# Splitting loads by pairs of heads and reordering the first units of an attention and mixture-of-depths kernel

## Chip, cores and metric

The kernel runs on one core of a Trainium2 chip. The metric is device time in microseconds; a kernel's time is the median of several executions. One further execution was taken with the hardware profiler, and every view below is of that one.

## What is computed

Eight batches, eight heads, 576 positions, head size 64. The first block is linear attention; the second takes the 128 positions of each batch with the highest gate score through an MLP and adds the result, scaled by the sigmoid of the score:

```python
q_s = softmax(q, axis=-1)                 # over the 64 features
k_s = softmax(k, axis=2)                  # over the 576 positions
x = einsum(q_s, k_s^T v)                  # 'bhsd,bhde->bhse'
x = x.transpose(0, 2, 1, 3).reshape(B, S, 512)
scores = x @ w_gate
out = x.copy()
for b in range(B):
    top = argpartition(-scores[b], 128)[:128]
    h = relu(x[b, top] @ w1)              # 512 -> 1024
    out[b, top] += sigmoid(scores[b, top])[:, None] * (h @ w2)
```

All tensors are float32.

## The kernel before

**Units.** Work is cut into 16 units: a unit is four heads (`qd` 0 or 1) of one batch, so batch b is units 2b and 2b+1. For each unit q, k and v come in by `load`, each as two DMAs: one of 5 rows of 64 values for each of 64 partitions and four heads (320 KB), one of 4 rows (256 KB). There are three buffers per tensor (`LD = 3`), so a unit's load waits until the unit three before has been used up. All loads but v of unit 0 are issued on SP's queue; the stores of attention rows (`x_store`, two DMAs) and the weights (`load_w1` four times 512 KB, `load_w2` twice 1 MB) are issued there too, in the order of the program.

**Steps of a unit.** `k_exp` (ACT), `v_copy` (POOL or DVE, into a tile that has a column of ones beside v), `kv_mm` (40 TensorE matmuls), `q_exp` (ACT, two halves, the first for heads 0 and 1), `kv_out` (DVE reciprocal, ACT copy, and DVE product and sum with the gate weights `wg`), `q_t` (two times ten transposes, each evicted from PSUM by ACT with a scale), `x_mm` (80 matmuls), `x_out` (DVE: reciprocal, scaling into `xs`, and the score columns into `sr`), `x_store`.

**Steps of a batch.** `score` adds up the columns; `score_row` turns the scores into a row on all partitions (five TensorE transposes, ACT copies); `compare` ranks them with five DVE instructions; `pick` makes the list of the 128 rows (DVE, TensorE) and gathers them from the stored output by an indirect DMA on POOL (`xr`); `gate`; `turn` transposes the gathered rows (four TensorE transposes, an ACT copy into `xT`); `mlp1` in eight pieces (with a relu on ACT after the fourth and the eighth); `mlp2` in eight pieces; `finish` adds and scatters.

**Order.** The order on each engine is the order of the program (`tc.manual_schedule()`). An opening loop over s = 0 to 3 (`EARLY = 4`) does the attention of units 0 to 3 and, with `kv_mm` and the exps of unit s + 1, prepares unit 4 as well. `fill(n)` puts n matmuls of ones between, whose result is not used. Batch 0's score, compare, pick, gate and turn are part of this loop or follow it directly. The main loop runs over s = 4 to 19; its step s holds attention of unit s, `kv_mm` of unit s + 1, and MLP pieces of batch (s - 4) // 2: mlp1 in even steps, mlp2 in odd ones. The pieces fill TensorE between the steps of a unit: two after `q_t`, one after `kv_mm`, four after `score_row`, and in odd steps one more after the next batch's `turn`. In an odd step, `pick` of the next batch comes after the first two pieces, and `turn` of it after the following five.

Of the kernel before, what the change touches and what calls it, by code (L numbers as in the profile page):

```python
# [17 lines left out]
def kernel(  # L18
# [62 lines left out]
    def part(i):  # L81
        return slice(64 * i, 64 * i + 64)
# [6 lines left out]
    LD = 3  # L89
    raw = {w: [const.tile([P, 4, R, D], F32, name=f"{w}{n}") for n in range(LD)] for w in "qkv"}  # L90

    def load(u, which, queue=nc.sync):
        b, qd = units[u]
        for what in which:
            src = {"q": q, "k": k, "v": v}[what]
            t = raw[what][u % LD]
            first = src[b, 4 * qd].offset
            for n, rows in ((1, N2), (0, R)):
                queue.dma_start(
                    out=t[n::2, :, :rows].rearrange("p h r d -> p h (r d)"),  # L100
                    in_=bass.AP(tensor=src.tensor, offset=first + n * R * D,
                                ap=[[9 * D, 64], [SD, 4], [1, rows * D]]))
# [19 lines left out]
    wg = const.tile([P, NQ, 2, D], F32, name="wg")  # L122
    for h in range(2):
        nc.scalar.dma_start(out=wg[part(h)].rearrange("p a i d -> p (a i) d"),
                            in_=bass.AP(tensor=moe_w_gate.tensor, offset=moe_w_gate.offset + h * D,
                                        ap=[[0, 64], [2 * D, 2 * NQ], [1, D]]))
# [39 lines left out]
    rest = const.tile([P, B * R], I32, name="rest")  # L166
    nc.gpsimd.iota(whole.rearrange("p (b r) -> p b r", b=B), pattern=[[2 * S, B], [2, R]], base=0, channel_multiplier=9)
    nc.gpsimd.iota(odd_p, pattern=[[0, 1]], base=0, channel_multiplier=1)
    vals = const.tile([P, B, R, NV], BF16, name="vals")
    valid_r = const.tile([P, 3, R], F32, name="valid_r")  # L170
    s_all = const.tile([P, B, R], F32, name="s_all")
# [21 lines left out]
    def k_exp(u):  # L193
        ke = at.tile([P, 4, R, D], F32, tag="ke", name="ke")
        nc.scalar.activation(out=ke, in_=raw["k"][u % LD], func=AF.Exp)  # L195
        st["ke", u] = ke

    def q_exp(u, i):
        if i == 0:
            st["qe", u] = at.tile([P, 2, R, 2, D], F32, tag="qe", name="qe")  # L200
        qr = raw["q"][u % LD].rearrange("p (i h) r d -> p i r h d", i=2)
        nc.scalar.activation(out=st["qe", u][:, i], in_=qr[:, i], func=AF.Exp)  # L202

    def v_copy(u, engine=nc.vector):
        engine.tensor_copy(out=v_ones[u % 2][:, :, :, :D], in_=raw["v"][u % LD])
# [25 lines left out]
    def q_t(u, i):  # L231
# [10 lines left out]
        nc.scalar.activation(out=st["qT", u][:, i].rearrange("p r a c -> p a r c"),  # L242
                             in_=t_ps[:, :, :R * 64].rearrange("p a (r c) -> p a r c", r=R),
                             func=AF.Copy, scale=krec[:, u, i:i + 1])

    def x_mm(u, i):

# [8 lines left out]

    xs, sr = {}, {}

    def x_out(u, i):
# [4 lines left out]
        x = st.pop(("x", u, i))[:, :, :R * C].rearrange("p h (r c) -> p h r c", r=R)  # L264
        rec = qrec[:, u, i].rearrange("p (h r) -> p h r", h=2)
        nc.vector.reciprocal(out=rec, in_=x[:, :, :, D])  # L266
        nc.vector.tensor_mul(xs[b][:, :, qd, i].rearrange("p r h d -> p h r d"), x[:, :, :, :D],  # L267
                             rec.to_broadcast([P, 2, R, D]))
        nc.vector.tensor_mul(sr[b][:, 2 * qd + i].rearrange("p (h r) -> p h r", h=2), x[:, :, :, D + 1], rec)

    def x_store(u):
        b, qd = units[u]
# [132 lines left out]
    def each(step, b, *args):  # L405
        for n in range(n_sl):
            step(b, n, *args)
# [84 lines left out]
    def load_w1(n):  # L492
        nc.sync.dma_start(out=w1[:, n], in_=moe_w1[n * P:(n + 1) * P])

    def load_w2(n):
        half = KF // 2
        nc.sync.dma_start(out=w2[:, n * half:(n + 1) * half],
                          in_=moe_w2[n * half * P:(n + 1) * half * P].rearrange("(f p) d -> p f d", p=P))
# [20 lines left out]

    for s in range(EARLY):  # L520
        q_t(s, 0)
        q_t(s, 1)
        k_exp(s + 1)
        v_copy(s + 1, nc.gpsimd)
        fill(2)
        x_mm(s, 0)
        x_mm(s, 1)
        fill(2)
        if s == 2:
            kv_mm(s + 1)  # L530
            q_exp(s + 1, 0)
            fill(3)
            pick(0)
            x_out(s, 0)
            kv_out(s + 1)
            x_out(s, 1)
            x_store(s)
            q_exp(s + 1, 1)
        else:
            x_out(s, 0)  # L540
            x_out(s, 1)
            x_store(s)
            if s == 1:
                score(0)
            kv_mm(s + 1)
            q_exp(s + 1, 0)
            kv_out(s + 1)
            if s == 1:
                score_row(0)
                for r in range(R):  # L550
                    compare(0, r)
            q_exp(s + 1, 1)
            if s == 3:
                score(1)
        fill(2)
        if s == 0:
            load_w1(0)
            load_w1(1)
        elif s == 1:
            load_w1(2)  # L560
            load_w1(3)
            load(4, "kvq")
            load(5, "kvq")
        else:
            load_w2(s - 2)
            load(s + 4, "kvq")
    each(gate, 0)
    each(turn, 0)

    number = None  # L570
    for s in range(EARLY, NU + LAG):

        mlp_b, odd = divmod(s - LAG, 2)
        piece = mlp2 if odd else mlp1
        f_next = 0

        def pieces(n):
            nonlocal f_next
            for _ in range(n):
                each(piece, mlp_b, f_next)  # L580
                f_next += 1

        here = s < NU
        after = s + 1 < NU
        last = s == NU - 1
        ends = s // 2 if here and odd else None
        compared = s // 2 - 1 if here and not odd else None
        chosen = (s - 3) // 2 if here and odd else B - 1 if s == NU else None
        if here:
            q_t(s, 0)  # L590
            q_t(s, 1)
        if after:
# [64 lines left out]
```

## Time and profile before

| | us |
|---|---|
| median of 3 runs (218.0 to 220.29) | 218.38 |
| the profiled execution | 217.89 |
| its span | 216.00 |
| TensorE busy | 197.5 (91%) |
| DVE busy | 116.2 (54%) |
| ACT busy | 88.6 (41%) |
| POOL busy | 34.4 (16%) |
| first MLP matmul starts | 42.64 |
| last MLP matmul ends | 208.8 |

DMA moved 46.81 MB, of which 41.36 MB went by SP's queue. In 40 equal slices of the span (5.4 us each) the mean busy share of the DMA engines, in tenths, and the rate:

```
DMA  5999999999999997958594949421313041101001
GB/s 179 299 356 358 375 398 369 362 392 377 377 384 381 375 344 249 314 157 283 171 320 154 313 133 303 161 82 49 113 52 109 7 156 52 49 3 52 5 5 52
```

A row of the views reads: source line, engine, operation, tile written and tiles read, shape. In a row of a timeline, the brackets at the end hold the engine's idle time before the instruction and what released it; "issue" means that it waited for nothing that the profile shows. PE is TensorE's matmul, PEld its weight load, and an engine's name with a q is its instruction sequencer, which issues DMAs.

### The profile page before, as it was taken

To read this page: it belongs to the slowest core of one execution; us is meant where nothing else is said; L and a number is where in the kernel's file an instruction comes from. 1 tells how busy PE (TensorE), PEld (TensorE's weight loads), DVE (VectorE), ACT (ScalarE), POOL (GpSimd) and SP (SyncE) were. 2 spreads that over 40 slices of the span, in tenths; PEclk is the share of its full clock that TensorE was granted. 3 is DMA by queue.
4 is the path that set the end of the run, shared out by engine and by line. 5 is a ranking of instruction groups with operands and counts; after the bars stand their busy time and mean duration, and the time that the engine had idled before them with its cause. 6 is when DMAs were issued, how large, how long until landed. Compare 5 with 4: busy or idle time off the path is not lost. (4 is left out here: it accounts for less than half of the span.)

```text
span 216.0 us, 7090 instructions
## 1 busy us (share of the span) xinstructions
PE 197.5 (91%) x3040; PEld 147.2 (68%) x3040; DVE 116.2 (54%) x359; ACT 88.6 (41%) x146; POOL 34.4 (16%) x78
## 2 busy tenths in 40 slices
PE   5987595999999999999999999999999989999960
PEld 2464462799749975897679776996599548749620
DVE  6552595668726774477626872596358665501010
ACT  2386374763626471746265443536263311211100
POOL 6022402300112012200320023001120112101010
PEclk9999999999999999999999999999999999999996
DMA  5999999999999997958594949421313041101001
GB/s 179 299 356 358 375 398 369 362 392 377 377 384 381 375 344 249 314 157 283 171 320 154 313 133 303 161 82 49 113 52 109 7 156 52 49 3 52 5 5 52
DMA packets 39335, 46.81 MB, mean 217 GB/s; under 512 B 2944, under 2 KB 36736, under 8 KB 39296
## 3 DMA queue, kind: packets, MB, share of 16 engines
q1 hardware_dynamic: 36928, 41.36, 56.4%
q0 software_dynamic: 1280, 4.20, 5.7%
q10 hardware_dynamic: 1088, 0.72, 1.1%
q8 instruction: 26, 0.43, 0.8%
q14 instruction: 13, 0.11, 0.2%
HBM read 34.73 MB, written 11.53 MB: 214 GB/s over the span
## 5 line engine op out<-in xcount | busy, mean ns | idle before, releaser
L382 PE MATMUL mm<-xT,w 128*128 128x128 f32 x512 | 62.1, 278 | 0.0
L382 PEld LDWEIGHTS mm<-xT,w 128*128 128x128 f32 x512 | 58.8, 192 | 2.3 <-ACT xT L370 1.5
L392 PE MATMUL mm<-w,hT 128*128 128x512 f32 x128 | 59.9, 603 | 0.0
L315 DVE SCALAR_TENSOR_TENSOR junk<-srow,s,not_before 128x576 bf16<-128x576 f32 x40 | 32.8, 819 | 8.3 <-ACT srow L307 7.2
L392 PEld LDWEIGHTS mm<-w,hT 128*128 128x128 f32 x128 | 22.5, 190 | 21.2 <-issue 20.4
L267 DVE TENSOR_TENSOR xs<-x,qrec 128x640 f32<-128x640 f32 x32 | 26.4, 825 | 1.1
L242 ACT ACTIVATE qT<-x,krec 128x640 f32<-128x640 f32 x32 | 23.9, 792 | 6.2 <-PE x L239 6.1
L400 DVE SCALAR_TENSOR_TENSOR o<-mm,g,xr 128x512 f32<-128x512 f32 x8 | 6.0, 751 | 37.7 <-PE mm L392 37.7
L202 ACT ACTIVATE qe<-q 128x640 f32<-128x640 f32 x32 | 23.6, 739 | 3.0 <-DMA q<-in_q_dram 2.8
L215 PE MATMUL tp<-v_ones,ke 128*64 128x65 f32 x640 | 22.6, 224 | 2.3 <-issue 2.1
L215 PEld LDWEIGHTS tp<-v_ones,ke 128*64 128x64 f32 x640 | 20.3, 137 | 5.3 <-issue 3.0
L253 PE MATMUL x<-kv_w,qT 64*64 64x66 f32 x1280 | 22.4, 221 | 0.0
L347 POOL DMA_INDIRECT xr<-out_dram,idx x8 | 8.0, 996 | 88.8 <-DVE qrec L266 72.6
L253 PEld LDWEIGHTS x<-kv_w,qT 64*64 64x64 f32 x1280 | 20.2, 134 | 2.6 <-ACT qT L242 0.8
L195 ACT ACTIVATE ke<-k 128x1280 f32<-128x1280 f32 x16 | 20.3, 1270 | 2.8 <-DMA k<-in_k_dram 2.8
L385 ACT ACTIVATE hT<-mm 128x512 f32<-128x512 f32 x16 | 9.5, 596 | 28.7 <-PE mm L382 28.7
L239 PEld LDWEIGHTS x<-ident,qe 64*128 64x128 f32 x320 | 11.7, 139 | 11.6 <-issue 5.0
L239 PE MATMUL x<-ident,qe 64*128 64x64 f32 x320 | 14.5, 229 | 4.9 <-issue 1.4
L266 DVE RECIPROCAL qrec<-x 128x10 f32<-128x10 f32 x32 | 6.9, 215 | 20.7 <-PE x L253 20.7
L401 POOL DMA_INDIRECT out_dram<-o,idx x8 | 10.1, 1269 | 46.8 <-DVE o L400 46.8
L226 ACT COPY kv_w<-tp 128x130 f32<-128x130 f32 x16 | 4.3, 266 | 31.4 <-DVE krec L224 31.4
L370 ACT COPY xT<-mm 128x512 f32<-128x512 f32 x8 | 4.7, 585 | 26.9 <-PE mm L368 26.9
(81 smaller groups left out, 126.0 us busy)
## 6 DMA issues: line engine op xcount, KB each, us to landing
k<-in_k_dram SPq DMA_DIRECT2D x16, 320.0 KB, 7.0
q<-in_q_dram SPq DMA_DIRECT2D x16, 320.0 KB, 6.1
out_dram<-xs SPq DMA_DIRECT2D x16, 320.0 KB, 2.9
v<-in_v_dram SPq DMA_DIRECT2D x15, 320.0 KB, 7.9
k<-in_k_dram SPq DMA_DIRECT2D x16, 256.0 KB, 7.2
q<-in_q_dram SPq DMA_DIRECT2D x16, 256.0 KB, 6.4
out_dram<-xs SPq DMA_DIRECT2D x16, 256.0 KB, 3.2
v<-in_v_dram SPq DMA_DIRECT2D x15, 256.0 KB, 7.7
```

The lines of the kernel that those rows point to most:

```text
L195: nc.scalar.activation(out=ke, in_=raw["k"][u % LD], func=AF.Exp)
L202: nc.scalar.activation(out=st["qe", u][:, i], in_=qr[:, i], func=AF.Exp)
L215: nc.tensor.matmul(out=kv[part(h), i], lhsT=ke[:, 2 * i + h, r], rhs=vo[:, 2 * i + h, r], start=(r == 0), stop=(r == N2))
L239: nc.tensor.transpose(out=t_ps[:, a, r * 64:(r + 1) * 64], in_=qe[part(a), i, r].rearrange("p h d -> p (h d)"), identity=ident[part(a), pa ...
L242: nc.scalar.activation(out=st["qT", u][:, i].rearrange("p r a c -> p a r c"), in_=t_ps[:, :, :R * 64].rearrange("p a (r c) -> p a r c", r= ...
L253: nc.tensor.matmul(out=x[part(c), h, r * C:(r + 1) * C], lhsT=qT[part(h), i, r, c], rhs=kv_w[u % 2][part(h), i], start=True, stop=True)
L267: nc.vector.tensor_mul(xs[b][:, :, qd, i].rearrange("p r h d -> p h r d"), x[:, :, :, :D], rec.to_broadcast([P, 2, R, D]))
L315: nc.vector.scalar_tensor_tensor(junk, st["srow", b], st["s", b][:, r:r + 1], not_before[:, r], op0=OP.subtract, op1=OP.is_ge, accum_out=s ...
L382: nc.tensor.matmul(out=h_ps[:, f % 4 * m:(f % 4 + 1) * m], lhsT=w1[:, d, f * P:(f + 1) * P], rhs=xT[:, d, :m], start=(d == 0), stop=(d == ...
L385: nc.scalar.activation(out=hT[:, f - 3:f + 1, :m], in_=h_ps[:, :4 * m].rearrange("p (f c) -> p f c", f=4), func=AF.Relu)
L392: nc.tensor.matmul(out=st["y", b, n][:m], lhsT=st["hT", b, n][:, f, :m], rhs=w2[:, f], start=(f == 0), stop=(f == KF - 1))
L401: nc.gpsimd.indirect_dma_start(out=out_rows[:(b + 1) * S], out_offset=bass.IndirectOffsetOnAxis(ap=idx[:m, :1], axis=0), in_=o[:m], in_off ...
```

## The change

Six things are changed.

1. `load` splits each DMA by pairs of heads: four per tensor and unit instead of two (`parts=2`), for all units but 0 and 1, which keep two (`parts=1`). k of unit 0 goes by ACT's queue and SP's, one DMA each; v of unit 0 moves to SP. The gate weights `wg` move from ACT's queue to POOL's. `WARM` is 18 instead of 20.
2. `q_t` can evict on DVE; the second half of units 0 and 1 does.
3. `x_out` is made of `x_sums` (reciprocal and score columns) and `x_scale`. For unit 1 the score columns and `score(0)` come first, then the scaling.
4. Stores ahead of weights: `load_w1` follows the stores of both unit 0 and unit 1; then come load 4, `load_w2`, load 5, and later the store of unit 2, load 6, the store of unit 3.
5. The opening loop no longer prepares unit 4. `turn(0)` comes inside step 3, ahead of unit 3's `x_out`.
6. In main steps 4 and 5 four pieces come first, then the exp of k, the copy of v (on DVE) and `kv_mm` and the rest of that same unit, its load of s + 3, and one piece; the one and the four pieces later in the step are left out there. Step 5 also prepares unit 6, as before.

```diff
-    WARM = 20
+    WARM = 18
-    def load(u, which, queue=nc.sync):
+    def load(u, which, queues=(nc.sync, nc.sync), parts=2):
...
-            first = src[b, 4 * qd].offset
-            for n, rows in ((1, N2), (0, R)):
-                queue.dma_start(
...
+            for heads in range(0, 4, 4 // parts):
+                first = src[b, 4 * qd + heads].offset
+                for n, rows in ((1, N2), (0, R)):
+                    queues[n].dma_start(
+                        out=t[n::2, heads:heads + 4 // parts, :rows].rearrange("p h r d -> p h (r d)"),
+                        in_=bass.AP(tensor=src.tensor, offset=first + n * R * D,
+                                    ap=[[9 * D, 64], [SD, 4 // parts], [1, rows * D]]))
...
-    load(0, "k")
-    load(0, "v", nc.scalar)
-    load(0, "q")
-    load(1, "kvq")
+    load(0, "k", (nc.scalar, nc.sync), 1)
+    load(0, "vq", parts=1)
+    load(1, "kvq", parts=1)
     load(2, "kvq")
...
-        nc.scalar.dma_start(out=wg[part(h)]...
+        nc.gpsimd.dma_start(out=wg[part(h)]...
...
+        if on_vector:
+            nc.vector.tensor_scalar(to, src, krec[:, u, i:i + 1], None, op0=OP.mult)
+        else:
+            nc.scalar.activation(out=to, in_=src, func=AF.Copy, scale=krec[:, u, i:i + 1])
...
     for s in range(EARLY):
         q_t(s, 0)
-        q_t(s, 1)
-        k_exp(s + 1)
-        v_copy(s + 1, nc.gpsimd)
+        q_t(s, 1, on_vector=s < 2)
+        if s + 1 < EARLY:
+            k_exp(s + 1)
+            v_copy(s + 1, nc.gpsimd)
         fill(2)
         x_mm(s, 0)
         x_mm(s, 1)
         fill(2)
...
+        elif s == 1:
+            x_sums(s, 0)
+            x_sums(s, 1)
+            score(0)
+            x_scale(s, 0)
+            x_scale(s, 1)
+            x_store(s)
             kv_mm(s + 1)
             q_exp(s + 1, 0)
+            kv_out(s + 1)
+            score_row(0)
+            for r in range(R):
+                compare(0, r)
             fill(3)
+            q_exp(s + 1, 1)
+            for n in range(KD):
+                load_w1(n)
+            load(4, "kvq")
+            load_w2(0)
+            load_w2(1)
+            load(5, "kvq")
+        elif s == 2:
+            kv_mm(s + 1)
+            q_exp(s + 1, 0)
+            fill(2)
             pick(0)
             x_out(s, 0)
             kv_out(s + 1)
             x_out(s, 1)
             x_store(s)
             q_exp(s + 1, 1)
+            load(6, "kvq")
         else:
+            each(turn, 0)
             x_out(s, 0)
             x_out(s, 1)
             x_store(s)
...
+            score(1)
+            each(gate, 0)
+    late = EARLY, EARLY + 1
...
+        if s in late:
+            pieces(4)
+            k_exp(s)
+            v_copy(s)
+            kv_and_exp(s)
+            load(s + 3, "kvq")
+            pieces(1)
+        after = after and s + 1 not in late
...
-        if s + 4 < NU:
+        if after and s + 4 < NU:
             load(s + 4, "kvq")
-        pieces(1)
+        if s not in late:
+            pieces(1)
...
-        pieces(4)
+        if s not in late:
+            pieces(4)
```

More of the change, by code (lines that the diff above doesn't have):

```diff
@@ L96, in load @@
             t = raw[what][u % LD]
-            first = src[b, 4 * qd].offset
-            for n, rows in ((1, N2), (0, R)):
[L99 to L102, printed above, removed]
+            for heads in range(0, 4, 4 // parts):
[5 more added lines that the diff above has]
+                                    ap=[[9 * D, 64], [SD, 4 // parts], [1, rows * D]]))
     ctx.enter_context(tc.manual_schedule())
@@ L120 @@
         nc.tensor.matmul(out=w_ps, lhsT=ones_b[:, :P], rhs=ones_b, start=True, stop=True)
[L122 to L126, printed above, removed]
     warm = const.tile([P, 1], F32, name="warm")
@@ L168 @@
     nc.gpsimd.iota(odd_p, pattern=[[0, 1]], base=0, channel_multiplier=1)
+    wg = const.tile([P, NQ, 2, D], F32, name="wg")
+    for h in range(2):
+        nc.gpsimd.dma_start(out=wg[part(h)].rearrange("p a i d -> p (a i) d"),
+                            in_=bass.AP(tensor=moe_w_gate.tensor, offset=moe_w_gate.offset + h * D,
+                                        ap=[[0, 64], [2 * D, 2 * NQ], [1, D]]))
     vals = const.tile([P, B, R, NV], BF16, name="vals")
@@ L229, in kv_out, with q_t @@
         nc.vector.reduce_sum(out=kw[:, :, D + 1], in_=prod, axis=AX.X)
-    def q_t(u, i):
+    def q_t(u, i, on_vector=False):
         if i == 0:
@@ L241, in q_t @@
                                     identity=ident[part(a), part(a)])
-        nc.scalar.activation(out=st["qT", u][:, i].rearrange("p r a c -> p a r c"),
-                             in_=t_ps[:, :, :R * 64].rearrange("p a (r c) -> p a r c", r=R),
-                             func=AF.Copy, scale=krec[:, u, i:i + 1])
+        to = st["qT", u][:, i].rearrange("p r a c -> p a r c")
+        src = t_ps[:, :, :R * 64].rearrange("p a (r c) -> p a r c", r=R)
+        if on_vector:
+            nc.vector.tensor_scalar(to, src, krec[:, u, i:i + 1], None, op0=OP.mult)
+        else:
+            nc.scalar.activation(out=to, in_=src, func=AF.Copy, scale=krec[:, u, i:i + 1])
     def x_mm(u, i):
@@ L257, with x_view, x_sums @@
     xs, sr = {}, {}
-    def x_out(u, i):
+    def x_view(u, i):
+        rec = qrec[:, u, i].rearrange("p (h r) -> p h r", h=2)
+        return st["x", u, i][:, :, :R * C].rearrange("p h (r c) -> p h r c", r=R), rec
+    def x_sums(u, i):
         b, qd = units[u]
@@ L263, in x_out, with x_scale @@
             sr[b] = md.tile([P, NQ * 2, G], F32, tag="sr", name="sr")
-        x = st.pop(("x", u, i))[:, :, :R * C].rearrange("p h (r c) -> p h r c", r=R)
-        rec = qrec[:, u, i].rearrange("p (h r) -> p h r", h=2)
+        x, rec = x_view(u, i)
         nc.vector.reciprocal(out=rec, in_=x[:, :, :, D])
+        nc.vector.tensor_mul(sr[b][:, 2 * qd + i].rearrange("p (h r) -> p h r", h=2), x[:, :, :, D + 1], rec)
+    def x_scale(u, i):
+        b, qd = units[u]
+        x, rec = x_view(u, i)
         nc.vector.tensor_mul(xs[b][:, :, qd, i].rearrange("p r h d -> p h r d"), x[:, :, :, :D],
                              rec.to_broadcast([P, 2, R, D]))
-        nc.vector.tensor_mul(sr[b][:, 2 * qd + i].rearrange("p (h r) -> p h r", h=2), x[:, :, :, D + 1], rec)
+    def x_out(u, i):
+        x_sums(u, i)
+        x_scale(u, i)
     def x_store(u):
@@ L528 @@
         fill(2)
-        if s == 2:
+        if s == 0:
+            x_out(s, 0)
+            x_out(s, 1)
+            x_store(s)
+            kv_and_exp(s + 1)
+            fill(2)
[5 more added lines that the diff above has]
+            x_scale(s, 1)
+            x_store(s)
             kv_mm(s + 1)
             q_exp(s + 1, 0)
+            kv_out(s + 1)
+            score_row(0)
+            for r in range(R):
+                compare(0, r)
             fill(3)
+            q_exp(s + 1, 1)
[8 more added lines that the diff above has]
+            q_exp(s + 1, 0)
+            fill(2)
             pick(0)
@@ L542 @@
             x_store(s)
[L543 to L568, printed above, removed]
+            score(1)
+            each(gate, 0)
+    late = EARLY, EARLY + 1
     number = None
```

## The prediction, made before the changed kernel was run

> **What bounds the kernel now.** I read the stretches first, then the timeline up to the first MLP matmul, then the issue durations on SP. Stretches (length, then busy time of each engine with its count, granted clock, DMA share, GB/s):
>
> ```profile
> 18.00:26.00 8.00, 4.56 (x136) 3.35 (x132) 2.77 (x10) 3.05 (x4) 3.07 (x7) 1.00 1.08 365
> 34.00:42.00 8.00, 5.91 (x156) 4.39 (x158) 5.36 (x18) 5.16 (x9) 2.39 (x2) 1.00 1.08 363
> 42.00:54.00 12.00, 11.97 (x229) 11.45 (x225) 8.58 (x27) 6.48 (x14) 0.99 (x5) 1.00 1.07 382
> ```
>
> There are two regimes. Up to 42 us no engine is full and the DMA engines are: attention units 0 to 3 run at the pace of loads. From 42 us TensorE has no gap to the end. So the end moves by what the first MLP matmul (T0, 42.64 us here) moves, plus all TensorE work and every TensorE wait added after it.
>
> The timeline (start, duration, and in brackets idle time before it with its releaser):
>
> ```profile
> 25.56 0.33 PE L215 MATMUL tp<-v_ones,ke 128*64 128x65 f32 x3 [2.09 <-issue]
> 27.39 0.82 DVE L315 SCALAR_TENSOR_TENSOR junk<-srow,s,not_before 128x576 bf16<-128x576 f32 x1 [0.34 <-ACT srow L307]
> 33.97 1.17 POOL L347 DMA_INDIRECT xr<-out_dram,idx  x1 [7.55 <-DVE qrec L266]
> 41.24 0.60 PE L368 MATMUL mm<-ident,xr 128*128 128x128 f32 x4
> 42.64 2.05 PE L382 MATMUL mm<-xT,w 128*128 128x128 f32 x16
> ```
>
> The chain into T0 is: kv of unit 2, score row, five compares (27.39 to 31.6), hit, gather, turn, MLP. The gather is issued at 33.97 and its landing is the long piece: xr landings run from 3.3 to 6.2 us, and this one takes the whole 6.2 under full DMA.
>
> SP's issues (min/median/max ns):
>
> ```profile
> L99 SPq DMA_DIRECT2D q<-in_q_dram x32: 601/602/1079, 2.4 to 132.2; - x32
> L274 SPq DMA_DIRECT2D out_dram<-xs x32: 601/634/1776, 21.0 to 173.5; - x32
> L493 SPq DMA_DIRECT2D w<-in_moe_w_dram x4: 552/818/993, 22.6 to 26.7; - x4
> L497 SPq DMA_DIRECT2D w<-in_moe_w_dram x2: 397/496/596, 40.8 to 49.6; - x2
> ```
>
> An issue costs about 0.6 us whether it moves 256, 320 or 512 KB; the least is 0.40, for 1 MB. It doesn't follow size.
>
> [...] at 365 GB/s a 288 KB transfer takes 0.81 us, its issue 0.64; halved, 0.40 against 0.64. [...] The 2.09 us above (and 1.35 at 19.42) are TensorE waiting with nothing to wait for while DMA is full[...]. [...]
>
> **The change, part by part.**
>
> *Split loads.* A unit is 6 issues now, and in an unhindered stretch they take 1.32+1.28+1.26 = 3.86 us for k, v, q, or 0.64 each. From unit 2 on it is 12. If a half costs as much to issue, a unit takes 12 x 0.64 = 7.7 us of SP, against 1.77 MB / 365 GB/s = 4.85 us of DMA. So SP, not DMA, paces loads: about 230 GB/s. Bounds: 0.40 an issue (row L497; then DMA stays the limit) to 0.66. I take 0.64, because four kinds of transfer of different sizes sit at 0.55 to 0.64. [...]
>
> *SP's order up to T0.* Units 0 and 1 stay whole, and SP already waits for earlier transfers to land there (1.5 us for v at 5.6 to 7.1), so v of unit 2 can land near 18.5 us (3.67 MB through q of unit 1 at 14.4, two tensors more at 365 GB/s, 1 us to land) instead of the 20.3 at which POOL copies it now. The trace keeps SP about eight transfers ahead of the landings (7 us to land at some 0.8 us apart), so q of unit 2 is issued as k of unit 2 lands, from 15.6 on, and its last issue ends at 18.2. Unit 3 then ends at 26, the stores of units 0 and 1 (4 issues, moved ahead of w1) at 28.6, w1 at 31. Its 2.1 MB need 5.7 us: landed at 36 to 37 (34.5 now).
>
> *Chain to the pick.* Second evictions of units 0 and 1 on VectorE: 0.82 there (row L267 reads the same 128x640 from PSUM), beside an idle DVE (1.92 us idle before qrec), and 0.75 saved in ACT's serial pair. Score columns first: two xs multiplies (2 x 0.82) leave the path, but TensorE still does kv of unit 2 before the score row[...]. With unit 2 at 18.5, POOL's copy 1.25, kv at about 21 to 22.3, the row 1.4 more: compares start near 24.2 (27.39 now) and end at 28.5; hit 0.85, 1.4 to the issue: 30.8. The gather reads stored rows, and the stores land only about 30.8, so they agree. While w1 streams I take 5.8 us to land (3.9 to 6.2): 36.6. Turn and copy, 1.6 (41.03 to 42.64 now): **T0 = 38.2**, 4.4 earlier; bounds 36.0 and 40.0.
>
> *Work moved behind T0.* kv of unit 4 (1.39) and its transposes (0.84) are done before 42.64 now, and come after T0: +2.23. kv of unit 5 only moves inside the full stretch.
>
> *Three new TensorE waits.* (1) In step 4, four mlp1 pieces come first; the fourth emits the relu on ACT, and the exp of k of unit 4 stands behind it. TensorE goes straight to kv of unit 4, and idles for relu 0.60 + exp 1.27 + about 0.35 of signals = 2.2 us (1.9 to 2.4). v_copy of unit 4 moves from POOL to DVE (0.82), under that exp. (2) Step 5 wants kv of unit 5 after four mlp2 pieces (4 x 0.91), but its v_copy on DVE stands behind the five compares of batch 1. From the end of x_mm of unit 4: DVE finishes x_out after 1.7, compares 5 x 0.865 = 4.3, copy 0.82, signal 0.15: 7.05. TensorE has score row 0.71, a piece 0.93, four pieces 3.65: 5.3. Wait 1.75 (1.4 to 2.1). (3) In step 5 the turn of batch 1 now follows the pick after only x_mm 1.40 and kv of unit 6 1.39, since the one and four pieces between them were used up earlier. From the pick's matmul: 1.4 to the gather's issue, 3.9 to 4.3 to land, against 0.27+1.40+1.39 = 3.06: wait 2.6 (1.7 to 4.7, landing 3.3 to 6.2). Behind the turn stand the last piece, finish, and all of step 6. Nothing recovers this, TensorE being full afterwards.
>
> *Costed at nothing.* wg through POOL: two issues at 4 to 6 us, beside loads; wanted at 11.37 by prod; without that cover up to 1 us on unit 0, which then waits for unit 1's loads anyway. Two warm matmuls fewer and k of unit 0 on two queues: k lands sooner, but DVE's v_copy starts at 7.50 behind constants as now. Loads 7 and 8 issued later: at 7.7 us a unit SP has unit 5 out by 47 and unit 6 by 56, wanted from about 56 on; unit 7 by 65, wanted at 73. In the steady stretch 12 x 0.64 + 1.3 = 9.0 us fit into 11.4. Moving w2 behind load 4: out by 40, wanted at 52.
>
> **Sum:** (38.2 - 42.64) + 2.23 + 2.2 + 1.75 + 2.6 = +4.3 us. The profiled execution is 217.89 (span 216.00 and 1.89 around it), so 222.2. The median of runs shown, 218.38, is 0.5 higher; I leave that.
>
> **Rivals.**
> - *The start is worth more than I give it (faster).* [...] If halves cost 0.40 to issue [...], bytes alone allow w1 at 31.4 (7.2 MB of loads, 1.2 of stores, 2.1 of w1 at 365 to 370 GB/s from 2.2 us, and 0.8), the gather is issued at 27 and lands at 30.9: T0 = 32.5. With wait (3) at 1.7: -10.1 + 2.23 + 2.2 + 1.75 + 1.7 = -2.3: 215.6. It decides the sign when T0 falls below 33.9. For it: the two waits on issue. Against: no issue of 256 to 512 KB took under 0.55.
> - *Gain and waits cancel.* T0 = 35.5 (issue near 0.5), waits at their low ends 1.9+1.4+2.0: -7.1 + 2.2 + 5.3 = +0.4: 218.3.
> - *The waits cost more.* T0 = 40 (gather issued at 32.5 and landing in 6.2), waits 2.4 + 2.1 + 4.0: +8.1: 226. [...]
> - *It doesn't do what it says:* the queues run in program order in this trace, so the moved steps move; no chance given.
>
> **Numbers.** My forecast has 0.47, the costly case 0.18, cancellation 0.22 and the faster start 0.13. Faster by over 1% (what these runs can tell from no change) needs under 216.2: 0.13. Slower by over 1% is over 220.6: forecast and costly case, and a little of the third: 0.67. Within: 0.20. The range runs from 217, below the cancelling case, to 226; it leaves out the faster start and the top of the costly case.
>
> **What would show it.** Issue rows of half loads at 0.6 us and DMA share below 0.9 between 20 and 30 us; the first mlp1 matmul near 38; in step 4 TensorE idle before kv, released by ke; in step 5 idle before kv, released by DVE's v_ones, and again before the turn, released by the landing of xr. I'm wrong if halves issue in 0.4 or less, if T0 is under 34, or if the waits are not there, because the engines' order differs from the program's.

## The result, and the profile after

The changed kernel takes 235.68 us (median of 4, 233.83 to 237.28) where the kernel before, run beside it, takes 219.33: a ratio of 1.0735, 95% interval 1.061 to 1.086. It is slower, as forecast, but by 16 us instead of 4. The profiled execution took 237.28 us, the longest of the four, with a span of 235.5.

Granted clock and DMA share in 40 equal slices of the span, in tenths:

```profile
PEclk9999997679999589999999999999999999999995
DMA  6996799799888798799969876997723130111001
```

Before, the clock was full until 212 us and the DMA row stood at 9 from 5 to 81 us. Now DMA is no longer full throughout, and TensorE falls to half clock twice between 36 and 50 us (for 3.41 us from 35.95 and for 6.83 from 42.78) and again from 77 to 84 (6.83 us from 76.91). The same three stretches as before (length, busy time and count of PE, PEld, DVE, ACT, POOL, clock, DMA share, GB/s):

```profile
18.00:26.00 8.00, 6.56 (x162) 4.60 (x164) 6.04 (x18) 4.84 (x9) 2.24 (x6) 1.00 0.66 181
34.00:42.00 8.00, 4.38 (x102) 3.25 (x104) 4.56 (x16) 2.38 (x4) 1.36 (x3) 0.79 0.99 344
42.00:54.00 12.00, 7.49 (x60) 6.93 (x62) 1.14 (x3) 3.07 (x5) 0.71 (x4) 0.72 0.84 270
```

From 18 to 26 us the loads move 181 GB/s; it was 365. TensorE, which had no gap from 42 us on, is busy for 7.49 of the 12 us after 42. The timeline of SP's queue shows what the loads wait for (start, duration of the group, count):

```profile
23.54 3.04 SPq L101 DMA_DIRECT2D v<-in_v_dram  x4
26.68 2.60 SPq L101 DMA_DIRECT2D q<-in_q_dram  x4
29.38 2.92 SPq L289 DMA_DIRECT2D out_dram<-xs  x4
32.34 2.98 SPq L508 DMA_DIRECT2D w<-in_moe_w_dram  x4
35.42 3.48 SPq L101 DMA_DIRECT2D k<-in_k_dram  x4
...
56.91 3.38 SPq L101 DMA_DIRECT2D q<-in_q_dram  x4
60.38 1.31 SPq L289 DMA_DIRECT2D out_dram<-xs  x2
...
67.17 3.31 SPq L101 DMA_DIRECT2D q<-in_q_dram  x4
70.58 1.31 SPq L289 DMA_DIRECT2D out_dram<-xs  x2
```

One group follows the other within 0.6 us, and mostly 0.1, from 17 to 80 us: SP has no time to spare. Until 36 us and after 58 almost all of it goes into the issues themselves. In between, the groups are longer than their issues: four half loads of v take 4.85 us from 51.96, and for 2.2 us of that (54.0 to 56.2) SP waits for transfers that it issued earlier. The stores of units 0 and 1 leave at 29.4, w1 at 32.3, and the store of unit 3 only at 70.6; before it was 46.4. What this does to the first batch, in the timeline of all engines:

```profile
29.43 1.25 POOL L206 COPY v_ones<-v 128x1280 f32<-128x1280 f32 x1 [7.08 <-DMA v<-in_v_dram]
30.73 1.39 PE L216 MATMUL tp<-v_ones,ke 128*64 128x65 f32 x40 [2.70 <-POOL v_ones L206]
32.50 0.27 PE L354 MATMUL tp<-vals,hit 128*128 128x5 bf16 x5
37.20 1.07 POOL L362 DMA_INDIRECT xr<-out_dram,idx  x1 [6.52 <-DVE xs L279]
43.99 1.09 PE L383 MATMUL mm<-ident,xr 128*128 128x128 f32 x4 [3.56 <-DMA xr<-out_dram,idx]
```

The compares ran from 24.23 to 28.50 and hit was there at 29.36. But the pick's matmul (32.50) stands behind kv of unit 3 (30.73), which waits for v of unit 3. Then the list is ready at 33.15, and the gather still isn't issued until 37.20, because the rows that it reads were stored late: the last store of unit 1 landed at 36.32. (The brackets name an instruction of DVE that writes `xs` for a later unit, which the gather doesn't read. POOL's queue had waited for the four stores until 36.32; with the stores on another queue, below, the gather follows its list.) From the first MLP matmul on, TensorE's own timeline has these waits, and one of 1.1 us near the end:

```profile
45.75 5.66 PE L397 MATMUL mm<-xT,w 128*128 128x128 f32 x32 [0.67 <-ACT xT L385]
53.26 1.39 PE L216 MATMUL tp<-v_ones,ke 128*64 128x65 f32 x40 [1.84 <-ACT ke L196]
66.69 1.39 PE L216 MATMUL tp<-v_ones,ke 128*64 128x65 f32 x40 [1.85 <-DVE v_ones L206]
80.26 1.12 PE L383 MATMUL mm<-ident,xr 128*128 128x128 f32 x4 [5.71 <-DMA xr<-out_dram,idx]
```

After the 0.67 us before T0 itself, they are the three that the prediction named, in its order and with its releasers. The 5.66 us of the first 32 matmuls, which take 3.84 at full clock in the run with whole loads below, are the low clock.

### The profile page after: what moved, and what is told of

Its sections match the earlier page's. It is cut to its first block, busy times and chain, and to the rows that moved or that the text cites. A ratio compares the mean times of both kernels' runs of the same rounds, so it can differ in the third digit from the quotient of the medians.

```text
span 235.5 us, 7207 instructions
## 1 busy us (share of the span) xinstructions
PE 199.3 (85%) x3026; PEld 150.0 (64%) x3034; DVE 119.1 (51%) x362; ACT 87.5 (37%) x144; POOL 34.5 (15%) x79
## 5 line engine op out<-in xcount | busy, mean ns | idle before, releaser
L397 PE MATMUL mm<-xT,w 128*128 128x128 f32 x512 | 64.2, 283 | 0.7 <-ACT xT L385 0.7
L397 PEld LDWEIGHTS mm<-xT,w 128*128 128x128 f32 x512 | 60.7, 197 | 3.2 <-ACT xT L385 2.4
L407 PE MATMUL mm<-w,hT 128*128 128x512 f32 x128 | 61.0, 610 | 0.0
L248 ACT ACTIVATE qT<-x,krec 128x640 f32<-128x640 f32 x30 | 22.4, 790 | 7.3 <-PE x L240 7.3
L257 PE MATMUL x<-kv_w,qT 64*64 64x66 f32 x1280 | 23.3, 225 | 0.3
L257 PEld LDWEIGHTS x<-kv_w,qT 64*64 64x64 f32 x1280 | 21.1, 138 | 3.2 <-ACT qT L248 1.5
```

The costliest lines, as they stand in the source:

```text
L248: nc.scalar.activation(out=to, in_=src, func=AF.Copy, scale=krec[:, u, i:i + 1])
L257: nc.tensor.matmul(out=x[part(c), h, r * C:(r + 1) * C], lhsT=qT[part(h), i, r, c], rhs=kv_w[u % 2][part(h), i], start=True, stop=True)
L397: nc.tensor.matmul(out=h_ps[:, f % 4 * m:(f % 4 + 1) * m], lhsT=w1[:, d, f * P:(f + 1) * P], rhs=xT[:, d, :m], start=(d == 0), stop=(d == ...
L407: nc.tensor.matmul(out=st["y", b, n][:m], lhsT=st["hT", b, n][:, f, :m], rhs=w2[:, f], start=(f == 0), stop=(f == KF - 1))
```

## Experiments

The theory after this reading: the split is the main loss. It makes SP's issues the pace, and everything queued on SP (stores, w1, the loads of later units) comes late; the three waits of the late place of units 4 and 5 add some 6 us. The rival: the new place of units 4 and 5 is the loss, and the split only feeds it. All kernels ran beside the kernel before, in sets of their own. In the last two sets (late_pick_first, w2late_fills, before_opening, and then pick_turn_first) the kernel before itself took 224.3 to 224.4 us, in the others 219.3 to 220.0, so between sets only ratios are compared.

| run | us | ratio to before (95%) | first MLP matmul |
|---|---|---|---|
| changed kernel | 235.7 | 1.074 (1.061 to 1.086) | 45.75 |
| whole_late | 228.1 | 1.038 (1.031 to 1.045) | 42.54 |
| split_old | 234.1 | 1.064 (1.057 to 1.072) | 50.85 |
| whole_old | 224.7 | 1.022 (1.013 to 1.031) | 46.64 |
| split_late_fills | 234.4 | 1.066 (1.055 to 1.076) | 46.03 |
| whole_old_w2late | 221.6 | 1.011 (1.000 to 1.021) | 43.89 |
| before_split | 232.4 | 1.059 (1.051 to 1.067) | 51.71 |
| split_late_poolstores | 232.9 | 1.060 (1.048 to 1.071) | 43.14 |
| whole_late_tuned | 225.1 | 1.024 (1.014 to 1.035) | 43.03 |
| late_pick_first | 234.7 | 1.043 (1.036 to 1.050) | 40.36 |
| w2late_fills | 224.6 | 0.998 (0.995 to 1.000) | 43.85 |
| before_opening | 224.1 | 1.001 (0.998 to 1.004) | 44.93 |
| pick_turn_first | 225.4 | 1.006 (1.004 to 1.009) | 43.29 |

### The split and the late place, crossed

By the late place the kernel is meant whose units 4 and 5 are prepared inside the MLP, by the old one that in which the opening loop prepares unit 4.

whole_late is the changed kernel with whole loads:

```diff
-    def load(u, which, queues=(nc.sync, nc.sync), parts=2):
+    def load(u, which, queues=(nc.sync, nc.sync), parts=1):
```

> The changed kernel with parts=1 everywhere: loads are whole again, all else as changed. Theory A (the split is the larger cost: SP's issue of 0.60 us per half paces loads, so v of unit 3, the stores and w1 come late, with them both gathers, and TensorE idles long enough to lose its clock): first mlp1 matmul near 38.5 us (45.75 in the changed kernel), v of unit 3 copied by 27, the gather of batch 1 issued within 0.5 us of its idx (3.5 after it in the changed kernel), 221 to 224 us. Theory B (the order with kv of units 4 and 5 inside the MLP is the larger cost, through its three TensorE waits): 229 us or more.

split_old keeps the split and puts unit 4 back into the opening loop; whole_old has both edits.

```diff
-        if s + 1 < EARLY:
-            k_exp(s + 1)
-            v_copy(s + 1, nc.gpsimd)
+        k_exp(s + 1)
+        v_copy(s + 1, nc.gpsimd)
...
         else:
-            each(turn, 0)
             x_out(s, 0)
             x_out(s, 1)
             x_store(s)
+            kv_and_exp(s + 1)
+            load(s + 4, "kvq")
             score(1)
+            fill(2)
             each(gate, 0)
+            each(turn, 0)
...
-    late = EARLY, EARLY + 1
+    late = ()
```

> The changed kernel with split loads, but with unit 4 prepared in the opening loop, turn(0) after it and main steps 4 and 5 in the order of the kernel before. Theory A: no TensorE wait within steps 4 and 5, but the first mlp1 matmul at 47 to 50 us, since kv of unit 4 waits for v of unit 4 (landed at 46.8 in the changed kernel); 225 to 229 us. Theory B: 222 us or less.

> Both of the two edits undone: whole loads, and units 4 and 5 in the order before; what is left are the two eviction engines, score columns first, stores ahead of weights, wg on POOL. Theory A: 8 to 12 us under split_old. Theory B: at most 3 us under split_old, and well under whole_late. Both: first mlp1 matmul at 39 to 41.5 us and 214.5 to 217 us, under the kernel before, as nothing of this part costs TensorE time later.

Taking the split away gains 7.6 us with the late place (235.7 to 228.1) and 9.4 with the old one (234.1 to 224.7). Taking the late place away gains 1.6 with the split, where the intervals of the two ratios overlap, and 3.4 without it. So the split is the larger part in both orders. whole_late fits neither of its theories, 221 to 224 or 229 and more: its v of unit 3 is copied by 25.6, as expected, but its first MLP matmul comes at 42.54 and not near 38.5. Without the split the compares start at 26.53 again, the pick (33.20) still stands behind kv of unit 3, and the gather takes 7.0 us to land. split_old missed its 225 to 229: with unit 4 in the opening loop TensorE stands 7.09 us for the v of unit 4 and 5.31 at kv of unit 5, since the split loads bring them late. The late place covers much of that. whole_old missed its 214.5 to 217 too, and this is the first sign of another loss: with both parts undone, 5.2 us remained.

### The split alone, in the kernel before

```diff
-    def load(u, which, queue=nc.sync):
+    def load(u, which, queue=nc.sync, parts=2):
...
+            for heads in range(0, 4, 4 // parts):
...
-    load(1, "kvq")
+    load(1, "kvq", parts=1)
```

> The kernel before with one edit: the loads of units 2 to 7 are split by pairs of heads, everything else stays. Theory A: the split costs by itself, since an issue takes 0.6 us whether it moves 128 or 256 KB, so SP paces the loads and a unit takes 7.2 to 8.7 us instead of 4.9: 226 us or more, with TensorE waiting for k or v of units 3 to 5. Rival B: the split only hurts because the stores and w2 were put in its way by the other parts of the change: at most 221.

It is theory A: one edit, ratio 1.059. The edit splits all loads from unit 2 on, as the changed kernel does, and not those of units 2 to 7 alone. The stretches of this kernel (first, and third of the three):

```profile
18.00:26.00 8.00, 7.20 (x179) 4.83 (x180) 5.38 (x17) 5.58 (x9) 2.24 (x6) 1.00 0.71 197
...
42.00:54.00 12.00, 7.73 (x94) 6.58 (x98) 2.26 (x9) 6.23 (x9) 2.24 (x6) 0.58 0.81 234
```

and its issues of q loads on SP (min/median/max ns):

```profile
L100 SPq DMA_DIRECT2D q<-in_q_dram x60: 601/605/1247, 2.4 to 161.4; - x60
```

Before, whole loads issued in 601/602 ns. Half the bytes issue in the same time, so 12 issues hold SP for 7.3 us or more (12 x 0.605), and from 18 to 26 us DMA runs at 197 GB/s and a share of 0.71, where the kernel before has 365 GB/s and 1.08. Timeline of SP's queue in the same run:

```profile
27.72 1.32 SPq L275 DMA_DIRECT2D out_dram<-xs  x2
29.09 1.49 SPq L494 DMA_DIRECT2D w<-in_moe_w_dram  x2
30.68 2.92 SPq L275 DMA_DIRECT2D out_dram<-xs  x2
33.64 1.43 SPq L494 DMA_DIRECT2D w<-in_moe_w_dram  x2
35.17 2.62 SPq L100 DMA_DIRECT2D k<-in_k_dram  x4
37.89 3.35 SPq L100 DMA_DIRECT2D v<-in_v_dram  x4
```

The store of unit 0 goes at 27.7 (21.0 before) and v of unit 4 at 37.9 (29.3 before). The list of batch 0 is ready at 31.21, sooner than the 33.68 of before, as the first loads do land sooner. But the gather is issued at 39.03, a microsecond after the last store of unit 1 landed (38.04), and v of unit 4 lands only at 45.0; its kv starts at 46.3 (39.5 before), and TensorE's turn follows at 49.5. What the split wins for unit 2 it loses several times over on everything that is queued behind it.

### The stores, and the pick behind kv

First the stores of units 0 to 5 on POOL's queue, then also the pick ahead of kv of unit 3:

```diff
-            nc.sync.dma_start(
+            (nc.gpsimd if u < 6 else nc.sync).dma_start(
```

> The changed kernel with one edit: the stores of units 0 to 5 are issued on POOL's queue instead of SP's. Theory A: in the changed kernel the stores stand behind twelve split loads on SP (the store of unit 3 is issued at 70.6 us, the gather of batch 1 only after it has landed, at 75.8, although its indices are there at 72.3). It expects the gather of batch 0 to be issued at 33.5 to 34.5 (37.2 in the changed kernel), the gather of batch 1 within about 1 us of its indices, the wait of TensorE for it to fall from 5.7 to about 2.6 to 3 us, and 227 to 231 us. Rival B: stores are not what the gathers wait for, or POOL's queue only moves the wait: 234 to 237.

```diff
+            pick(0)
             kv_mm(s + 1)
             q_exp(s + 1, 0)
             fill(2)
-            pick(0)
```

> The changed kernel with the stores of units 0 to 5 on POOL's queue (232.9, first MLP matmul at 43.14 us) and one more edit: the pick of batch 0 stands ahead of kv of unit 3 on TensorE instead of behind it. Theory A: in the changed kernel the pick was ready at 29.4 and stood until 32.5 behind a kv that waited for v of unit 3, and this is one of the two things that made the first MLP matmul late, the stores being the other. It expects the pick at 29.5 to 30.5, the gather issued at 31 to 32 and landed at 37 to 38; the turn then waits for the x matmuls of unit 3 and no more for the gather, so the first MLP matmul comes at 40 to 41.5, and the time is 229.5 to 231.5. Rival B: v of unit 3 sets the pace anyway, because the x matmuls of unit 3 stand ahead of the turn and end at 41 to 42 whatever the pick does: first MLP matmul at 42.5 or later, 232 to 234.

The gathers do what was expected of theory A. Timeline of split_late_poolstores:

```profile
34.93 1.06 POOL L362 DMA_INDIRECT xr<-out_dram,idx  x1 [4.16 <-DVE qrec L273]
...
69.14 0.28 PE L354 MATMUL tp<-vals,hit 128*128 128x5 bf16 x5 [1.77 <-DVE hit L350]
...
74.62 0.65 PE L383 MATMUL mm<-ident,xr 128*128 128x128 f32 x4 [2.37 <-DMA xr<-out_dram,idx]
```

The gather of batch 0 follows its list by 0.3 us, and the third wait falls from 5.71 to 2.37 us, near the 2.6 of the prediction. The time, 232.9, lies between the two expectations, and the interval of its ratio overlaps that of the changed kernel; 1.77 us comes back as a new wait of the pick of batch 1 for hit, and the pick of batch 0 comes later than in the changed kernel (33.9 after 32.5). With the pick first as well, TensorE's timeline of late_pick_first reads:

```profile
29.39 0.28 PE L354 MATMUL tp<-vals,hit 128*128 128x5 bf16 x5 [1.38 <-DVE hit L350]
30.50 1.58 PE L216 MATMUL tp<-v_ones,ke 128*64 128x65 f32 x40 [0.83 <-POOL v_ones L206]
...
39.08 0.60 PE L383 MATMUL mm<-ident,xr 128*128 128x128 f32 x4
40.36 3.84 PE L397 MATMUL mm<-xT,w 128*128 128x128 f32 x32 [0.68 <-ACT xT L385]
```

The gather is issued at 30.61, where the prediction had 30.8, but lands only at 38.18. The first MLP matmul comes at 40.36: 5.4 us of its delay were the two places where something stood in a queue. The ratio of 1.0433, put on the kernel before of the earlier set (219.96), is 229.5, the lower end of what was expected of theory A; its interval just overlaps that of split_late_poolstores (1.048 to 1.071). As the two runs are of different sets, only the time of the first matmul is compared between their traces.

### The clock

```diff
+            fill(10)
             kv_mm(s + 1)
             q_exp(s + 1, 0)
             fill(2)
             pick(0)
+            fill(6)
...
+            fill(14)
             each(turn, 0)
```

and 24 more matmuls of ones before the turn of batch 1.

> The changed kernel with unused matmuls of ones where TensorE idles: 10 before kv of unit 3, 6 after the pick of batch 0, 14 before turn(0), 24 before the turn of batch 1 (0.21 us each at full clock). They keep TensorE busy and leave what it waits for. If the slow clock is a cost of its own (mlp1 took 5.66 us for 32 matmuls of the profile where 3.7 is the rate at full clock): granted clock 1.00 until the end, 231 to 232.5 us. If not: no change, 234 to 237 us.

Within the work the clock is then full but for one stretch, 46.3 to 49.7, in which the first MLP matmuls still take 5.47 us; its mean over the span is 0.987 instead of 0.953. The rest after them is 2.4 us shorter in the traces, the median 1.3 us, less than its uncertainty. The median is where no change was expected (234 to 237). So the slow clock accounts for a microsecond or two, not for the loss.

### The three waits

whole_late_tuned is whole_late with w2 where the kernel before has it, and in steps 4 and 5 of the main loop the exp of k and the copy of v (on POOL) ahead of the pieces; in step 5 one piece stands ahead of kv, and three are kept for the time before the turn.

```diff
         if s in late:
-            pieces(4)
             k_exp(s)
-            v_copy(s)
+            v_copy(s, nc.gpsimd)
+            pieces(1 if odd else 4)
...
+        elif odd:
+            pieces(3)
```

> The run with whole loads and the new place of units 4 and 5 (228.1), with two things altered: w2 back where the kernel before has it, and in the first two steps of the main loop the exp of k and the copy of v (on POOL again) stand ahead of the MLP pieces instead of behind four of them, with pieces left over for the time before kv and before the turn of batch 1. Theory A: the three new waits (exp of k behind the relu, v copy behind five compares, turn right behind the pick) are what the new place costs, and w2 early costs the start: the waits fall to at most 1 us together, the first MLP matmul comes at 41 to 42.5, and the time is 219 to 222. Rival B: the waits only move to other places, or w2 isn't the cause of the late start: 225 to 229.

```profile
56.83 1.39 PE L216 MATMUL tp<-v_ones,ke 128*64 128x65 f32 x40 [1.03 <-issue]
```

Wait 1 is gone. In place of wait 2 TensorE stands 1.03 us before kv of unit 5: the exp of its k, which comes after a relu on ACT, ends only 0.1 us before that kv starts. A further 0.68 us goes to an exp of q, and the third wait is 1.26 us instead of 2.17. Together that is 2.97 us where whole_late has 1.85 + 1.75 + 2.17 = 5.77, and not the 1 us expected. From the first MLP matmul to the end it took 180.2 us instead of 183.4. So the waits cost some 3 us that another order of the same work saves, if none of it is w2's. The first MLP matmul stayed at 43.0, though, with the pick behind kv of unit 3 again (33.42), and 225.1 is what Rival B expected. It doesn't reach whole_old_w2late below, which has the old place of units 4 and 5.

### What remained: w2, the dummy matmuls, the rest of the opening

whole_old_w2late moves w2 back:

```diff
             load(4, "kvq")
-            load_w2(0)
-            load_w2(1)
             load(5, "kvq")
...
+            load_w2(0)
             load(6, "kvq")
...
+            load_w2(1)
             load(s + 4, "kvq")
```

> The run with whole loads and the old place of unit 4 (224.7, first MLP matmul at 46.6 us), with w2 put back where the kernel before has it: its first half after the query exponentials of unit 3, ahead of load 6, its second half one opening step later, ahead of load 7. Theory A: what was left of the loss (+5.2 us against the kernel before) is w2's 2 MB taking the DMA engines at 34 to 42 us[...]. It then expects the gather of batch 0 to land in about 6.2 us instead of 7.8, the first MLP matmul at 41 to 42.5, and 217 to 220 us. Rival B: w2 is not the cause (the new order of stores, weights, evictions or the gate weights on POOL is): 223 to 226, first MLP matmul at 45 or later.

It took 221.6, 3.1 us less than whole_old (the intervals of the ratios overlap, 1.013 to 1.031 and 1.000 to 1.021). The time lies between the two expectations, and the first MLP matmul moved by 2.8 us, not by the 4 or 5 expected. In whole_old TensorE's timeline has

```profile
37.62 1.32 PE L257 MATMUL x<-kv_w,qT 64*64 64x66 f32 x73
41.24 0.34 PE L257 MATMUL x<-kv_w,qT 64*64 64x66 f32 x7 [2.30 <-issue]
...
42.43 2.44 PE L216 MATMUL tp<-v_ones,ke 128*64 128x65 f32 x40
```

with a wait for nothing that the profile shows in the middle of 80 matmuls, then kv at half clock. With w2 late that wait is gone, the gather lands in 7.1 instead of 7.8 us, and v of unit 5 is copied by 44.8 instead of 50.4. So w2's place carries most of this remainder by the traces; what the 2.30 us waited for isn't shown.

In two more runs, w2late_fills puts back dummy matmuls of the kernel before around the pick, and before_opening is the kernel before with only the evictions on VectorE and the score columns first.

```diff
-            fill(2)
+            fill(3)
             pick(0)
...
             q_exp(s + 1, 1)
+            fill(2)
             load_w2(0)
```

> The run with whole loads, the old place of unit 4 and w2 late (221.6, first MLP matmul at 43.89 us) with the dummy matmuls of the kernel before put back around the pick of batch 0: three instead of two ahead of it and two behind it. Theory A: without these two TensorE was idle for 1.7 and 1.1 us with 0.5 us of work between, fell to half clock from 34.3 to 41.2, and the x matmuls, fills and kv of units 3 and 4 took 2.2 us longer. It expects a clock of 1.00 to the end, the first MLP matmul at 41.3 to 42.3, and 219 to 220.3 us. Rival B: the clock doesn't matter there, since the turn waits for something else [...]: first MLP matmul at 43 or later, 221 to 222.5.

> The kernel before with two parts of the change alone: the second eviction of units 0 and 1 on VectorE, and in the second opening step the sums and the score columns ahead of the two multiplies of xs, which come before the store. Theory A: these parts do what the prediction gave them, the compares start some 1 us earlier than 27.4 us and the gather is issued that much earlier; since it lands 6.2 to 7 us later and kv of unit 4 and the fills stand ahead of the turn, little of it reaches the first MLP matmul: 41.5 to 42.6 us, and 217.5 to 219.5, no change that can be told. Rival B: they gain as much as they move, the gather lands at 39 and the first MLP matmul comes by 41.3: 216 to 217.3. Rival C: a later store of unit 1 holds the gather back: above 220.

before_opening is at 1.001: these two parts, made alone, change nothing that can be told. The way to it was not the one expected: the compares start at 27.28, hardly sooner than the 27.39 of before, and the first MLP matmul comes at 44.93, not at 41.5 to 42.6. w2late_fills is at 0.998, level with the kernel before, so what is left of the change costs nothing on balance once the split, the place of units 4 and 5, w2 and these dummy matmuls are undone. The parts left, stores ahead of w1 and the gate weights on POOL among them, weren't run one by one. The expected mechanism isn't shown, however: its profiled run still had half clock from 36.1 to 39.5, and its first MLP matmul at 43.85. That the dummies are worth the last per cent rests on two ratios from different sets.

The last run tried to beat both kernels by moving TensorE's order on from w2late_fills:

```diff
+            pick(0)
+            fill(2)
             kv_mm(s + 1)
             q_exp(s + 1, 0)
-            fill(3)
-            pick(0)
...
             x_store(s)
+            each(turn, 0)
             kv_and_exp(s + 1)
...
-            each(turn, 0)
```

> The run with w2 late and the fills put back (0.998 of the kernel before), with two moves on TensorE: the pick of batch 0 ahead of kv of unit 3, and the turn of batch 0 ahead of kv of unit 4. Theory A: in that run the pick stood 1.7 us behind kv of unit 3 (hit 31.2, pick 32.95) and the turn stood 2 us after the gather had landed (40.5, 42.45) behind kv of unit 4 and two fills; taken away, this brings the gather's issue to 32.3 and its landing to 39, the first MLP matmul comes before or right after kv of unit 4, and the time falls by 1 to 2.5 us, to a ratio of 0.988 to 0.996 against the kernel before: faster, by little. Rival B: TensorE's order was not the limit there, since what moves ahead only pushes kv back and TensorE does the same work after it: ratio 0.996 to 1.003. Rival C: with the pick first TensorE waits for hit ahead of kv of unit 3, and the delay of kv of units 3 and 4 costs more than the gather gains: above 1.003.

```profile
31.59 0.28 PE L354 MATMUL tp<-vals,hit 128*128 128x5 bf16 x5 [1.39 <-DVE hit L350]
...
39.68 0.63 PE L383 MATMUL mm<-ident,xr 128*128 128x128 f32 x4 [0.59 <-DMA xr<-out_dram,idx]
40.24 1.39 PE L216 MATMUL tp<-v_ones,ke 128*64 128x65 f32 x40
...
43.29 2.05 PE L397 MATMUL mm<-xT,w 128*128 128x128 f32 x16
```

The lines are TensorE's timeline of pick_turn_first. The gather is issued at 32.54 and landed at 39.54, as expected, but TensorE now stands 1.39 us for hit and 0.59 for the gather, and does kv of unit 4 after the turn instead of before it. The ratio is 1.006 (1.004 to 1.009): Rival C. No version run here is shown to beat the kernel before.

## Why the prediction went wrong

By its steps, against the profiled execution (237.28 us, 15.1 above the predicted 222.2). T0 is the start of the first MLP matmul.

| step | predicted | measured | adds to 222.2 |
|---|---|---|---|
| the issue of a half load, us | 0.64 | 0.60 to 0.64 | |
| compares start, end | 24.2, 28.5 | 24.23, 28.50 | |
| gather of batch 0 issued | 30.8 | 37.20 | |
| first MLP matmul (T0) | 38.2 | 45.75 | +7.6 |
| wait 1, exp of k behind the relu | 2.2 | 1.84 | -0.4 |
| wait 2, v copy behind the compares | 1.75 | 1.85 | +0.1 |
| wait 3, turn of batch 1 | 2.6 | 5.71 | +3.1 |
| low clock after T0 | none | 3.5 | +3.5 |
| TensorE waits for DVE near the end (206 us) | none | 1.1 | +1.1 |

The low clock is worked out as 5.66 - 3.84 us for the first 32 MLP matmuls, plus 1.70 for the turn of batch 1 (1.12 for 0.60), two mlp2 pieces (1.92 for 1.02) and the transposes after them (1.12 for 0.84). The moved work is 1.39 and 0.84 us in this trace too, the 2.23 of the prediction. The rows add up to 15.0 of the 15.1.

**What was right.** The direction; that an issue doesn't follow size, so that SP paces the loads; unit 2 earlier and the compares to within 0.1 us; the three waits with their places and releasers, two of them within 0.4 us. (The terms of wait 2 add up to 7.0 and not 7.05, so it was 1.7 by its own sum. The 0.35 us of signals in wait 1 was an estimate: in the trace the relu starts 0.04 us after the matmuls, kv 0.05 after the exp, and the exp 0.1 before the relu ends.) The early compares came with the split: they start at 24.00 in before_split, and at 27.28 with the evictions and the score columns alone. In whole_late the part after T0 took 10.1 us more than before, where the prediction had 8.8 (2.23 + 2.2 + 1.75 + 2.6); that it comes so near is in part luck, as the three waits were 0.8 shorter there and a wait of 1.53 us near the end, which the prediction lacks, made up for it.

**The step that failed: T0 = 38.2, which was 45.75.** It read "hit 0.85, 1.4 to the issue: 30.8 ... the stores land only about 30.8, so they agree". Two queues are missing in it. On TensorE the pick stands behind kv of unit 3, and the sentence goes from hit to the issue as if the engine were free; the price of this was 2.8 us (43.14 to 40.36). And on SP the stores were put too early. Unit 3's last issue ended at 29.3, not 26, because q of unit 2 ended at 20.8 instead of 18.2 and the next 12 issues took 8.4 us instead of 7.7; and the last store landed 4.0 us after the end of its issue (32.30 to 36.32), where the working had 2.2 (28.6 to 30.8). This was 2.6 us (45.75 to 43.14), of which 0.5 is the turn at half clock (1.09 for 0.60). The remaining 2.2 in T0 are the gather, 7.6 instead of 5.8 us to land, above the upper bound taken (6.2), and 0.9 us behind the x matmuls of unit 3, less 0.5 for an issue 0.2 sooner and a turn 0.3 shorter.

**Wait 3** failed by the same omission: its gather also reads stored rows, and the store of unit 3 stood behind the split loads of units 4 to 6. "At 7.7 us a unit SP has unit 5 out by 47 and unit 6 by 56" was costed at nothing, because the loads were wanted later. They left by 60.3 and 70.5, and what came late was not the loads but the store behind them. Moved to POOL's queue, it leaves a wait of 2.37 us, beside the new one of 1.77 at the pick.

**Costed at nothing and not nothing:** w2 behind load 4, "out by 40, wanted at 52". What counted was not when w2 is wanted but what its 2 MB stand ahead of: some 3 us in whole_old, by the traces. The dummy matmuls that the change drops around the pick were not in the working at all.

**The clock** is not in the sum. Half clock cost 1.70 us of TensorE's work behind the gap of 5.71 us, and 1.8 us in the first MLP matmuls. That a late T0 would bring the latter wasn't considered, since T0 was expected early. The length of a single gap is no sign of half clock in these traces: the changed kernel's first half clock, at 35.95, comes with gaps of 1.66 and 1.13 us and 0.5 us of work between them, while after a single gap of 2.65 us in whole_old, which ends at 25.51, three matmuls of ones take 0.81 us (0.82 before, at a clock of 1.00). In the changed kernel TensorE was idle for 2.4 to 2.7 of the 3.41 us before each of the three falls within its work (35.95, 42.78, 76.91); nothing run here tells how much idle time is enough.

## What to carry to other kernels

SP's queue, which paced the loads here, delayed everything else that was queued on it (the store of unit 3 left at 70.6 us, before at 46.4). So when a transfer is split, the stores, weights and later loads behind it are to be followed on that queue to their last reader, a gather of stored rows among them, and not the split loads alone. "Wanted at" is no measure of a moved transfer; ask what stands behind it. And before a chain of times is written down, name for each link what its engine has ahead of it in program order.

## What the runs showed of the hardware

- **The price of an issue on SP didn't follow size.** Loads of q issue in 602 ns at the median where they move 256 and 320 KB, and in 605 where they move 128 and 160; on POOL's queue two stores took 1.32 to 1.36 us, the same again. In the changed kernel SP's issues were the limit, and taking the stores off SP shows in what DMA moves: with them on POOL's queue 256 GB/s instead of 181 from 18 to 26 us (share 0.85 instead of 0.66), and T0 at 43.14 instead of 45.75.
- **The indirect gather of 128 rows landed late while DMA was full, and by how much varied.** Batch 0's took from 5.4 us (before_split) to 7.8 (whole_old); before it took 6.2 at a DMA share of 1.07, in the changed kernel 6.7 at 1.00, where the medians of all eight gathers are 3.9 and 4.5. Issuing it sooner didn't bring it forward by as much: 6.6 us of earlier issue (37.20 to 30.61 in late_pick_first) brought 5.7 of earlier landing. The time of issue didn't decide it alone, as whole_old (34.0, 7.8 us) and w2late_fills (33.9, 6.6 us) show, which differ in w2's place and dummy matmuls.
- **TensorE's waits for nothing that the profile shows** went with the fullness of DMA. In every run with whole loads (DMA share 1.08 from 18 to 26 us in the kernel before) one of them falls near 25 us in the middle of a row of equal matmuls: 2.09 us before, 1.63 to 2.65 in the others. In every run with split loads (0.66 in the changed kernel, 0.71 in before_split) it is at most 0.5 us. With the split they get shorter; what they wait for isn't shown, and no run tested the cause by itself.
